# An earlier start for the tokens, a warm-up and split key folds in an attention and mixture-of-experts kernel

## Chip, cores and metric

One core of one Trainium2 chip. Times are device microseconds of one execution; lower is better. TensorE is called PE, VectorE DVE, ScalarE ACT, GpSimd POOL; SP is the engine that only issues transfers.

## What is computed

A transformer block on 2048 tokens of width 512, all in float32:

```python
h  = x + LinearAttention(layernorm(x)) @ wo
h2 = h + MoE(layernorm(h))            # top-1 of 8 experts, width 1792, silu
# attention, for each of 32 heads of width 16:
phi(q) = concat(softmax(q @ w_phi), softmax(-(q @ w_phi)))   # the same for k
o = phi_q @ (phi_k^T V) / (phi_q @ sum(phi_k))
# MoE: out = sum_e gate_e * silu(x @ w1[e]) @ w2[e] for the one expert with the largest logit;
# the softmax over that single logit is 1
```

## The kernel before

Tokens come in 16 tiles of 128. Each float32 product is made of three matmuls in a faster format: every operand is split into a high part (`hi_of`, a rounding copy on ACT, L69) and a low part (`lo_of`, a subtraction on DVE, L72), and `mm3` (L75 to L77) adds hi·hi, hi·lo and lo·hi. A split is therefore one ACT and one DVE instruction, and PE waits for both.

**Stage 1, weights.** `w_phi` is folded into the query and key weights: `fold` (L300) makes, for each of four row blocks `dt`, four full float32 matmuls into one PSUM bank `pf` (in the trace each is two records) and then splits that bank into `wkhi` and `wklo` (or `wqhi`, `wqlo`). Value weights (`split_w` into `wvhi`, `wvlo`) and output weights (`wohi`, `wolo`) are only split, with the gate's columns beside them. Raw weights are loaded in two halves each (`load_w`, L297) on SP's queue, in this order: w_phi, key weights, first tokens, gate, value weights, second tokens, query weights, output weights, transposed output weights.

**Stage 2, tokens.** For tile `c`: `s_ln` loads it (`load_x`, L216) and normalises it (DVE statistics L220 and L221, POOL for the reciprocal root, ACT for `xn`, L230); `s_tr` transposes it on PE (L235, into `pt`) and splits it (`xh`, `xl`); `s_k`, `s_v` and `s_q` project it; `feat1` and `feat2` make the two softmaxes (DVE, ACT, and on POOL the product `ph`, L352); `s_kv` accumulates phi_k^T V, `s_qt` transposes the query features into `phT` (L375 and L376). The last two tiles' query features are finished in the next stage.

**Stage 3, attention output and routing**, a loop over `c` (L562) in which each step works on four tiles at different depths: `s_num` (pn, L265), `s_ot` (pto), `s_wo` (po), routing ranks, and from `c` = 12 on the splits of the first expert's weights. `fq` of tiles 14 and 15 is made at `c` = 2 and 3, and their `s_qt` runs at `c` = 3 and 4.

**Stage 4, experts**: units of 128 tokens, each with its expert's weights loaded, split and multiplied.

The order on each engine is set by a scheduler that takes the written program and moves independent instructions; `tc.issue_after(ins)` keeps instructions of the same engine behind `ins` in that order, and makes no wait between engines. Pools hand out buffers in turn: `ps` has four PSUM banks for `bank(...)` tiles, `psw` one double bank for `pv` and `po`.

Of the kernel before, what the change touches and what calls it, by code (L numbers as in the profile page):

```python
# [9 lines left out]
F32 = mybir.dt.float32  # L10
# [4 lines left out]
AF = mybir.ActivationFunctionType  # L15
# [6 lines left out]
P = 128  # L22
# [19 lines left out]
def kernel(  # L42
# [22 lines left out]
    def mid(ap, n):  # L65
        return ap.unsqueeze(1).to_broadcast([ap.shape[0], n] + list(ap.shape[1:]))

    def hi_of(dst, src):
        A.activation(dst, src, AF.Copy)  # L69

    def lo_of(dst, src, hi):
        V.tensor_tensor(dst, src, hi.bitcast(F32), op=OP.subtract)  # L72

    def mm3(ps, ahi, alo, bhi, blo, first, last):
        T.matmul(ps, ahi, bhi, start=first, stop=False)  # L75
# [45 lines left out]
    def bank(name):  # L121
        return ps.tile([P, 512], F32, name=name, tag="b")
# [65 lines left out]
    with ExitStack() as actx:  # L188
# [22 lines left out]
        def row(name, bufs, tag):  # L211
            return work.tile([P, D], F32, name=name, tag=tag, bufs=bufs)

        def load_x(c):
            st[c]["xt"] = row("xt", 3, "xt")
            nc.sync.dma_start(st[c]["xt"], x[c * P:(c + 1) * P, :])  # L216

        def ln_rstd(src, mv, rstd):
            bs = work.tile([P, 6], F32, name="bs")
# [9 lines left out]
            G.tensor_scalar(nb, mean, rstd, -1.0, op0=OP.mult, op1=OP.mult)  # L229
            A.activation(dst, src, AF.Identity, bias=nb, scale=rstd)  # L230

        def transpose4(src, name):
            pt = bank(name)
            for k in range(KD):
                T.transpose(pt[:, k * P:(k + 1) * P], src[:, k * P:(k + 1) * P], ident)  # L235
            return pt.rearrange("p (k t) -> p k t", k=KD)
# [42 lines left out]
        if True:  # L279
# [15 lines left out]
            def load_w(i, src):  # L295
                for j in range(2):
                    nc.sync.dma_start(stage[i][j], src[j * 256:(j + 1) * 256].rearrange("(t p) d -> p t d", p=P))  # L297
                return stage[i]

            def fold(w_raw, whi, wlo):  # L300
                for dt in range(KD):
                    pf = bank("pf")
                    for t in range(4):
                        T.matmul(pf[:, t * P:(t + 1) * P], w_raw[t // 2][:, t % 2, dt * P:(dt + 1) * P],
                                 wphi_s[:, t, :], start=True, stop=True)
                    hi_of(whi[:, dt, :], pf)
                    lo_of(wlo[:, dt, :], pf, whi[:, dt, :])

            def split_w(w_raw, gate, whi, wlo):
                for t in range(KD):  # L310
# [7 lines left out]
                    lo_of(wlo[:, :, i, v], gate[:, :, i, :], whi[:, :, i, v])  # L318

            def s_ln(c):  # L320
                load_x(c)
                xt = st[c]["xt"]
                mv = work.tile([P, 2], F32, name="mv", bufs=4)
                rstd = work.tile([P, 1], F32, name="rstd", bufs=4)
                std = work.tile([P, 1], F32, name="std", bufs=4)
                ve = ln_rstd(xt, mv, rstd)
                G.tensor_tensor(std, ve, rstd, op=OP.mult)
                st[c]["std"], st[c]["mv"] = std, mv
                st[c]["xn"] = row("xn", 3, "xn")
                normalise(st[c]["xn"], xt, mv[:, 0:1], rstd)  # L330

            def s_tr(c):
                st[c]["x"] = split_t(transpose4(st[c]["xn"], "pt"))
# [22 lines left out]

            def s_v(c):
                p = proj2(st[c]["x"], wvhi, wvlo, "pv")
                A.activation(v17[c % 3].rearrange("p (i h) f -> p i h f", i=2)[:, :, :, 0:DH],
                             p[:, :, 0:D // 2].rearrange("p i (h f) -> p i h f", f=DH), AF.Copy)  # L360
                A.activation(xwg[:, c], p[:, :, D // 2:HC], AF.Copy, scale=st[c]["std"])

# [7 lines left out]
            def s_qt(c):  # L370
                ph = st[c]["fq"]
                for i in range(2):
                    pt = bank("ptq")
                    for g in range(4):
                        T.transpose(pt[:, g * P:(g + 1) * P], ph[:, (4 * i + g) * P:(4 * i + g + 1) * P], ident)  # L375
                    A.activation(phT[c][:, 4 * i:4 * i + 4, :], pt.rearrange("p (g t) -> p g t", g=4), AF.Copy)  # L376

            nc.sync.dma_start(wphi_s, wphi.rearrange("t p f -> p t f"))
            wk_raw = load_w(0, wqkT[D:2 * D])
            s_ln(0)  # L380
            nc.sync.dma_start(wgs, wg.rearrange("(t p) e -> p t e", p=P))
            wv_raw = load_w(1, wv)
            s_ln(1)
            wq_raw = load_w(2, wqkT[0:D])
            wo_raw = load_w(3, wo)
            for i in range(3):
                V.memset(v17[i][:, :, DH:DH + 1], 1.0)
            fold(wk_raw, wkhi, wklo)
            woT_raw = load_w(0, woT)
            s_tr(0)  # L390
            split_w(wv_raw, wgs.rearrange("p t (i e) -> p t i e", i=2), wvhi, wvlo)
            pc = bank("pcs")
            for k in range(KD):
                T.matmul(pc[:, 0:E], onesf, wgs[:, k, :], start=(k == 0), stop=(k == KD - 1))
            wgc = wp.tile([P, KD, E], F32, name="wgc")
            csg = wp.tile([P, E], F32, name="csg")
            V.tensor_scalar(csg, pc[:, 0:E], 1.0 / D, None, op0=OP.mult)
            V.tensor_tensor(wgc, wgs, mid(csg, KD), op=OP.subtract)

            def s_k(c):  # L400
                return proj(st[c]["x"], wkhi, wklo, "pk")
# [4 lines left out]
            for c in range(NT - 1):  # L406
                pk = s_k(c)
                if c:
                    st[c - 1]["fq"] = feat2(st[c - 1]["tq"])
                tk = feat1(pk)  # L410
                s_v(c)
                if c == 0:
                    fold(wq_raw, wqhi, wqlo)
                if c == 3:
                    pg = bank("pog")
                    for dt in range(KD):
                        for t in range(4):
                            T.matmul(pg[:, dt * E:(dt + 1) * E], woT_raw[t // 2][:, t % 2, dt * P:(dt + 1) * P],
                                     wgc[:, t, :], start=(t == 0), stop=(t == 3))
                    split_w(wo_raw, pg[:, 0:KD * E].rearrange("p (t i e) -> p t i e", t=KD, i=2), wohi, wolo)  # L420
                if c + 2 < NT:
                    s_ln(c + 2)
                s_tr(c + 1)
                if c == NT - 2:
                    st[c]["fk"] = feat2(tk)
                    tk = feat1(s_k(NT - 1))
                    s_v(NT - 1)
                    s_kv(c - 1)
                    s_qt(c - 1)
                    st[NT - 1]["fk"] = feat2(tk)  # L430
                    pq = [proj(st[i]["x"], wqhi, wqlo, "pq") for i in (NT - 2, NT - 1)]
                else:
                    pq = proj(st[c]["x"], wqhi, wqlo, "pq")
                    st[c]["fk"] = feat2(tk)
                    st[c]["tq"] = feat1(pq)
                    if c:
                        s_kv(c - 1)
                        s_qt(c - 1)
# [123 lines left out]
        for c in range(NT + 8):  # L562
            if c > 1:
                at(s_num, c)
                at(s_ot, c - 1)
            if c in (2, 3):
                st[NT - 4 + c]["fq"] = feat2(st[NT - 4 + c]["tq"])
            if c in (3, 4):
                s_qt(NT - 5 + c)
            if c == 5:  # L570
                c1.close()
                mw = ctx.enter_context(tc.tile_pool(name="mw", bufs=1, reuse_waits="tile"))
                raw.extend(mw.tile([P, CW], F32, name=f"raw{i}") for i in range(4))
            at(s_wo, c - 2)
            b, j = divmod(c - 3, NB)
            if j == NB - 1:
                at(s_inv, b - 1, NT // NB)
                if b == NT // NB // 2:
                    s_first()
                at(s_top, b, NT // NB)  # L580
                if b == NT // NB // 2 - 1:
                    s_star()
                    late[0].close()
                    mwb = ctx.enter_context(tc.tile_pool(name="mwb", bufs=1, reuse_waits="tile"))
                    first_expert(mwb)
# [273 lines left out]
```

## Time and profile before

| | us |
|---|---|
| median of three runs (lowest to highest) | 724.08 (721.95 to 724.55) |
| the profiled execution, its own time | 722.81 |
| its span, first to last instruction | 721.0 |
| PE busy in the span | 697.6 |
| DVE busy | 450.6 |
| ACT busy | 324.2 |
| POOL busy | 171.7 |

The profile is one execution. Busy time of an engine is the time in which at least one of its instructions ran; idle time is put down to what ended it. A matmul's record is longer than the step to the next one, since matmuls overlap; the step between starts is its price in a stream. The clock column is the share of PE's full clock that was granted; before the first recorded change of the clock it shows 1.00.

### The profile page before, as it was taken

How to read it: one execution, taken by the hardware profiler on the slowest of the kernel's cores; microseconds unless marked ns; L12 is line 12 of the kernel's file. 1: busy time of each engine (PE TensorE's matmuls, PEld its weight loads, DVE VectorE, ACT ScalarE, POOL GpSimd, SP SyncE). 2: the span in 40 equal slices, each digit the busy share in tenths (PEclk: the TensorE clock that was granted, in tenths of full speed). 3: DMA queues.
4: the chain of work that ended last, by engine and by line, in shares of the span. 5: the costliest groups of instructions: out<-in, count | busy, mean ns of one | idle time of the engine just before them, and what ended most of it. 6: DMA issues, size and time to landing. Idle time of an engine off the chain costs nothing. (4 is left out here: it accounts for less than half of the span.)

```text
span 721.0 us, 12308 instructions
## 1 busy us (share of the span) xinstructions
PE 697.6 (97%) x4130; PEld 606.6 (84%) x4130; DVE 450.6 (63%) x886; ACT 324.2 (45%) x522; POOL 171.7 (24%) x271
## 2 busy tenths in 40 slices
PE   5999999999999999879999999999999999999996
PEld 5889998989999999758888888888888888888885
DVE  3987888777785679784422999972284563922211
ACT  3544444443324347442112888861284553822211
POOL 2255535433315435531110011111011111011110
PEclk9999999999999999999999999999999999999999
DMA  8210101000002249318400799981065481001000
GB/s 310 85 30 31 45 15 30 15 30 1 1 2 74 74 141 398 136 44 310 174 31 7 278 362 396 359 349 36 15 239 218 145 320 32 1 29 31 30 31 5
DMA packets 21910, 87.59 MB, mean 121 GB/s; under 512 B 3071, under 2 KB 3583, under 8 KB 14657
## 3 DMA queue, kind: packets, MB, share of 16 engines
q1 hardware_dynamic: 18624, 76.86, 29.1%
q0 software_dynamic: 3200, 9.75, 4.0%
q8 instruction: 34, 0.56, 0.3%
q14 instruction: 52, 0.42, 0.2%
HBM read 78.18 MB, written 9.21 MB: 121 GB/s over the span
## 5 line engine op out<-in xcount | busy, mean ns | idle before, releaser
L72 DVE TENSOR_TENSOR wlo<-raw,whi 128x1024 fp32r<-128x1024 f32 (+1 forms) x120 | 135.9, 1151 | 15.8 <-ACT whi L69 8.1
L69 ACT ACTIVATE whi<-raw 128x1024 fp32r<-128x1024 f32 (+1 forms) x120 | 118.1, 1001 | 60.4 <-PE mh L77 43.6
L75 PE MATMUL mh<-whi,xhi 128*128 128x512 f32 (+1 forms) x304 | 114.6, 377 | 0.2 <-ACT xhi L69 0.2
L76 PE MATMUL mh<-wlo,xhi 128*128 128x512 f32 (+1 forms) x304 | 111.2, 366 | 0.0
L77 PE MATMUL mh<-whi,xlo 128*128 128x512 f32 (+1 forms) x304 | 111.2, 366 | 0.0
L76 PE MATMUL my<-wlo,hThi 128*128 128x512 f32 x266 | 104.9, 394 | 3.5 <-DVE wlo L72 3.3
L75 PE MATMUL my<-whi,hThi 128*128 128x512 f32 x266 | 107.7, 405 | 0.2 <-ACT hThi L69 0.2
L77 PE MATMUL my<-whi,hTlo 128*128 128x512 f32 x266 | 104.7, 394 | 0.3 <-DVE hTlo L72 0.3
L803 POOL DMA_INDIRECT out_dram<-yo,sidx x19 | 21.5, 1131 | 347.9 <-DVEq L640 198.9
L72 DVE TENSOR_TENSOR hTlo<-mtr,hThi 128x512 fp32r<-128x512 f32 x76 | 47.0, 621 | 88.7 <-ACTq L640 54.9
L163 ACT ACTIVATE hs<-mh 128x512 f32<-128x512 f32 x76 | 41.0, 540 | 132.4 <-PE mh L77 132.4
L352 POOL TENSOR_TENSOR ph<-t,sm 128x1024 f32<-128x1024 f32 x32 | 62.1, 1941 | 79.4 <-DVE sm L350 39.4
L77 PEld LDWEIGHTS mh<-whi,xlo 128*128 128x128 f32 x304 | 57.0, 188 | 10.3
L75 PEld LDWEIGHTS mh<-whi,xhi 128*128 128x128 f32 x304 | 57.1, 188 | 9.9 <-ACT xhi L69 0.5
L76 PEld LDWEIGHTS mh<-wlo,xhi 128*128 128x128 f32 x304 | 57.2, 188 | 9.3
L76 PEld LDWEIGHTS my<-wlo,hThi 128*128 128x128 f32 x266 | 50.3, 189 | 14.4 <-DVE wlo L72 4.1
L802 DVE SCALAR_TENSOR_TENSOR yo<-my,xg 128x512 f32<-128x512 f32 x19 | 14.2, 748 | 75.2 <-PE my L77 75.2
L77 PEld LDWEIGHTS my<-whi,hTlo 128*128 128x128 f32 x266 | 50.2, 189 | 11.1 <-DVE hTlo L72 0.5
L75 PEld LDWEIGHTS my<-whi,hThi 128*128 128x128 f32 x266 | 50.3, 189 | 9.9 <-ACT hThi L69 0.5
L69 ACT ACTIVATE hThi<-mtr 128x512 fp32r<-128x512 f32 x76 | 41.1, 542 | 11.7 <-PE mtr L732 11.6
L349 DVE TENSOR_REDUCE sm<-t 128x64 f32<-128x1024 f32 x32 | 38.8, 1214 | 10.3 <-ACT t L344 10.3
L344 ACT ACTIVATE t<-t 128x1024 f32<-128x1024 f32 x32 | 33.9, 1060 | 21.3 <-DVE t L343 17.3
(209 smaller groups left out, 1382.1 us busy)
## 6 DMA issues: line engine op xcount, KB each, us to landing
raw<-in_w_dram SPq DMA_DIRECT2D x56, 1024.0 KB, 5.3
xt<-in_x_dram SPq DMA_DIRECT2D x32, 256.0 KB, 2.8
hbuf<-hb SPq DMA_DIRECT2D x8, 516.0 KB, 3.2
phT<-in_wqkT_dram SPq DMA_DIRECT2D x4, 512.0 KB, 6.9
phT<-in_wv_dram SPq DMA_DIRECT2D x2, 512.0 KB
phT<-in_wo_dram SPq DMA_DIRECT2D x2, 512.0 KB, 8.4
phT<-in_woT_dram SPq DMA_DIRECT2D x2, 512.0 KB, 6.9
xg<-hbuf,gidx POOLq DMA_INDIRECT x21, 3.8
```

Source lines behind the costliest of these rows:

```text
L69: A.activation(dst, src, AF.Copy)
L72: V.tensor_tensor(dst, src, hi.bitcast(F32), op=OP.subtract)
L75: T.matmul(ps, ahi, bhi, start=first, stop=False)
L76: T.matmul(ps, ahi, blo, start=False, stop=False)
L77: T.matmul(ps, alo, bhi, start=False, stop=last)
L163: A.activation(hs[c % 2][:, 0:fw], p[:, 0:fw], AF.Silu)
L344: A.activation(t, t, AF.Exp)
L349: V.tensor_reduce(sm, t, AX.X, OP.add)
L352: G.tensor_tensor(ph.rearrange("p (a f) -> p a f", f=DH), t, bc(sm, DH), op=OP.mult)
L802: V.scalar_tensor_tensor(y, py, g[:, D + 2:D + 3], g[:, 0:D], op0=OP.mult, op1=OP.add)
L803: G.indirect_dma_start(out=out, out_offset=bass.IndirectOffsetOnAxis(ap=sidx[:, u:u + 1], axis=0), in_=y, in_offset=None, bounds_check=S - ...
```

## The change

1. The first two token tiles are loaded on ACT's queue, ahead of everything else; SP's queue begins with w_phi and the key weights.
2. PE runs 28 transposes of the identity matrix into an unused bank (`warm`).
3. The key weights are folded in two halves, one for each half of the load: all four `dt` for the first half, then the transposes and split of the first token tile (in the `psw` bank), then all four `dt` for the second half with the splits.
4. The value splits, the second tile's normalisation and what belongs to the gate are kept behind the last key split on ACT and on DVE. Their loads are on SP and are not held.
5. The output weights' splits are kept behind the copy of the third tile's `v` on ACT.
6. `s_qt` of tiles 14 and 15 runs at `c` = 4 and 5.

```diff
-        def load_x(c):
+        def load_x(c, queue=nc.sync):
             st[c]["xt"] = row("xt", 3, "xt")
-            nc.sync.dma_start(st[c]["xt"], x[c * P:(c + 1) * P, :])
+            queue.dma_start(st[c]["xt"], x[c * P:(c + 1) * P, :])
...
+            def fold_half(w_raw, pf, dt, i):
+                for t in (2 * i, 2 * i + 1):
+                    T.matmul(pf[:, t * P:(t + 1) * P], w_raw[i][:, t % 2, dt * P:(dt + 1) * P],
+                             wphi_s[:, t, :], start=True, stop=True)
+
+            def fold_split(pf, dt, whi, wlo):
+                return hi_of(whi[:, dt, :], pf), lo_of(wlo[:, dt, :], pf, whi[:, dt, :])
...
             def s_ln(c):
-                load_x(c)
+                if c > 1:
+                    load_x(c)
...
+            load_x(0, nc.scalar)
+            load_x(1, nc.scalar)
+            s_ln(0)
             nc.sync.dma_start(wphi_s, wphi.rearrange("t p f -> p t f"))
             wk_raw = load_w(0, wqkT[D:2 * D])
-            s_ln(0)
-            nc.sync.dma_start(wgs, wg.rearrange("(t p) e -> p t e", p=P))
-            wv_raw = load_w(1, wv)
-            s_ln(1)
-            wq_raw = load_w(2, wqkT[0:D])
-            wo_raw = load_w(3, wo)
+            warm = bank("warm")
+            for i in range(28):
+                T.transpose(warm[:, i % 4 * P:(i % 4 + 1) * P], ident, ident)
...
-            fold(wk_raw, wkhi, wklo)
-            woT_raw = load_w(0, woT)
-            s_tr(0)
-            split_w(wv_raw, wgs.rearrange("p t (i e) -> p t i e", i=2), wvhi, wvlo)
...
+            pf = [bank("pf") for _ in range(KD)]
+            for dt in range(KD):
+                fold_half(wk_raw, pf[dt], dt, 0)
+            st[0]["x"] = split_t(transpose4(st[0]["xn"], "pt", psw.tile([P, 2, 512], F32, name="pt0", tag="w")[:, 0, :]))
+            for dt in range(KD):
+                fold_half(wk_raw, pf[dt], dt, 1)
+                hi, lo = fold_split(pf[dt], dt, wkhi, wklo)
+            with tc.issue_after(hi.ins), tc.issue_after(lo.ins):
+                nc.sync.dma_start(wgs, wg.rearrange("(t p) e -> p t e", p=P))
+                wv_raw = load_w(1, wv)
+                split_w(wv_raw, wgs.rearrange("p t (i e) -> p t i e", i=2), wvhi, wvlo)
+                s_ln(1)
+                wq_raw = load_w(2, wqkT[0:D])
+                wo_raw = load_w(3, wo)
+                woT_raw = load_w(0, woT)
...
-                    split_w(wo_raw, pg[:, 0:KD * E].rearrange("p (t i e) -> p t i e", t=KD, i=2), wohi, wolo)
+                    with tc.issue_after(st[2]["v"].ins):
+                        split_w(wo_raw, pg[:, 0:KD * E].rearrange("p (t i e) -> p t i e", t=KD, i=2), wohi, wolo)
...
-            if c in (3, 4):
-                s_qt(NT - 5 + c)
+            if c in (4, 5):
+                s_qt(NT - 6 + c)
```

More of the change, by code (lines that the diff above doesn't have):

```diff
@@ L68, in hi_of @@
     def hi_of(dst, src):
-        A.activation(dst, src, AF.Copy)
+        return A.activation(dst, src, AF.Copy)
     def lo_of(dst, src, hi):
-        V.tensor_tensor(dst, src, hi.bitcast(F32), op=OP.subtract)
+        return V.tensor_tensor(dst, src, hi.bitcast(F32), op=OP.subtract)
     def mm3(ps, ahi, alo, bhi, blo, first, last):
@@ L230, in normalise, with transpose4 @@
             A.activation(dst, src, AF.Identity, bias=nb, scale=rstd)
-        def transpose4(src, name):
-            pt = bank(name)
+        def transpose4(src, name, pt=None):
+            pt = bank(name) if pt is None else pt
             for k in range(KD):
@@ L302, in fold @@
                     pf = bank("pf")
[L303 to L307, printed above, removed]
+                    fold_half(w_raw, pf, dt, 0)
+                    fold_half(w_raw, pf, dt, 1)
+                    fold_split(pf, dt, whi, wlo)
             def split_w(w_raw, gate, whi, wlo):
@@ L358, in s_v @@
                 p = proj2(st[c]["x"], wvhi, wvlo, "pv")
-                A.activation(v17[c % 3].rearrange("p (i h) f -> p i h f", i=2)[:, :, :, 0:DH],
+                st[c]["v"] = A.activation(v17[c % 3].rearrange("p (i h) f -> p i h f", i=2)[:, :, :, 0:DH],
                              p[:, :, 0:D // 2].rearrange("p i (h f) -> p i h f", f=DH), AF.Copy)
@@ L385 @@
-            wo_raw = load_w(3, wo)
+            warm = bank("warm")
+            for i in range(28):
+                T.transpose(warm[:, i % 4 * P:(i % 4 + 1) * P], ident, ident)
             for i in range(3):
                 V.memset(v17[i][:, :, DH:DH + 1], 1.0)
-            fold(wk_raw, wkhi, wklo)
-            woT_raw = load_w(0, woT)
-            s_tr(0)
-            split_w(wv_raw, wgs.rearrange("p t (i e) -> p t i e", i=2), wvhi, wvlo)
-            pc = bank("pcs")
-            for k in range(KD):
-                T.matmul(pc[:, 0:E], onesf, wgs[:, k, :], start=(k == 0), stop=(k == KD - 1))
@@ L395 @@
[L395 to L398, printed above, removed]
+            pf = [bank("pf") for _ in range(KD)]
+            for dt in range(KD):
+                fold_half(wk_raw, pf[dt], dt, 0)
+            st[0]["x"] = split_t(transpose4(st[0]["xn"], "pt", psw.tile([P, 2, 512], F32, name="pt0", tag="w")[:, 0, :]))
@@ new lines @@
+            for dt in range(KD):
[9 more added lines that the diff above has]
+                woT_raw = load_w(0, woT)
+                pc = bank("pcs")
+                for k in range(KD):
+                    T.matmul(pc[:, 0:E], onesf, wgs[:, k, :], start=(k == 0), stop=(k == KD - 1))
+                wgc = wp.tile([P, KD, E], F32, name="wgc")
+                csg = wp.tile([P, E], F32, name="csg")
+                V.tensor_scalar(csg, pc[:, 0:E], 1.0 / D, None, op0=OP.mult)
+                V.tensor_tensor(wgc, wgs, mid(csg, KD), op=OP.subtract)
```

## The prediction

> **What bounds the kernel now.** I read the page first, then the list of what TensorE (PE) waited for, then the start in order of time, then busy time by stretch.
>
> ```profile
> PE 697.6 (97%) x4130; PEld 606.6 (84%) x4130; DVE 450.6 (63%) x886; ACT 324.2 (45%) x522; POOL 171.7 (24%) x271
> ```
>
> ```profile
> PE pf L304 <- DMA phT<-in_wqkT_dram: 6.7, 2, 5.5
> PE my L76 <- DVE wlo L72: 3.3, 1, 3.3
> PE po L75 <- DVE lg L467: 2.6, 2, 2.1
> PE ptq L375 <- POOL hb L461: 1.4, 1, 1.4
> PE pt L235 <- DVE wklo L72: 1.0, 1, 1.0
> ```
>
> PE is the bound: 697.6 of 721.0 us. Its idle time stands in a few places, and the change touches three of them: the first wait for the key weights (6.7 us), the first transpose (1.0) and the late query transpose (1.4). What is gained there reaches the end only if PE is full from there on.
>
> ```profile
> 25.00:27.50 2.50, 2.50 (x18) 2.27 (x18) 2.50 (x5) 2.14 (x4) 0.00 (x0) 1.00 0.00 0
> 27.50:30.00 2.50, 2.30 (x10) 1.54 (x10) 2.50 (x7) 0.00 (x0) 0.97 (x3) 1.00 0.00 0
> 50.00:60.00 10.00, 10.00 (x79) 9.46 (x77) 9.25 (x15) 4.66 (x7) 3.99 (x6) 1.00 0.04 5
> ```
>
> Columns: stretch, its length, busy us (count) of PE, PEld, DVE, ACT, POOL, PE clock, DMA share, GB/s. Up to 30 us VectorE (DVE) is as full as PE, so the start is a race of two engines. Later PE alone is full (50 to 60), though DVE has little to spare. The waits listed for 30 to 200 us are nil, so what the start gains is carried to there one for one.
>
> Now the start itself, in order of time (start, length, engine, line, tiles, count):
>
> ```profile
> 1.27 0.29 POOL masks.py:199 TENSOR_SCALAR_AFFINE_SELECT ident<-ident 128x128 f32<-128x128 f32 x1
> 5.51 2.04 PE L304 MATMUL pf<-wphi_s,phT 128*128 128x128 f32 x8 [5.51 <-DMA phT<-in_wqkT_dram]
> 8.78 4.62 PE L304 MATMUL pf<-wphi_s,phT 128*128 128x128 f32 x24 [1.22 <-DMA phT<-in_wqkT_dram]
> 9.52 0.69 DVE L220 BATCH_NORM_STATS2 bs<-xt 128x6 f32<-128x512 f32 x1 [7.36 <-DMA xt<-in_x_dram]
> 12.29 0.81 ACT L230 ACTIVATE xn<-xt,nbias,rstd 128x512 f32<-128x512 f32 x1 [2.36 <-POOL nbias L229]
> 13.01 2.04 ACT L69 ACTIVATE wkhi<-pf 128x512 fp32r<-128x512 f32 x4
> 14.37 0.66 PE L235 MATMUL pt<-ident,xn 128*128 128x128 f32 x4 [0.97 <-DVE wklo L72]
> 17.28 1.90 DVE L72 TENSOR_TENSOR wvlo<-phT,wvhi 128x512 fp32r<-128x512 f32 x3
> 19.62 0.39 PE L77 MATMUL pk<-wkhi,xl 128*128 128x512 f32 x1
> 22.60 3.29 PE L304 MATMUL pf<-wphi_s,phT 128*128 128x128 f32 x28
> 29.20 0.40 PE L77 MATMUL pq<-wqhi,xl 128*128 128x512 f32 x1
> 29.44 0.39 PE L75 MATMUL pk<-wkhi,xh 128*128 128x512 f32 x1
> 32.24 0.28 PE L75 MATMUL pv<-wvhi,xh 128*128 128x260 f32 x1
> 32.36 0.28 PE L76 MATMUL pv<-wvlo,xh 128*128 128x260 f32 x1
> ```
>
> Three things are seen. The key weights land in halves, at 5.5 and 8.8 us, and the first tokens at 9.5, behind them. The fold (L304; each matmul of the program is two records) costs 2.04/8 = 0.25 us a record at first, 0.19 in the second burst, and 3.29/28 = 0.12 later: the early records run on about half the clock, though the clock column (1.00) doesn't show it before 12 us. And tokens and key weights come ready together only at 13 to 14 us. A split, projection and fold step starts every 0.51 us on ACT (2.04/4), 0.60 on DVE (1.90 for three), 0.24 on PE for 512 columns (29.20 to 29.44) and 0.12 for 260 (32.24 to 32.36).
>
> **The change, part by part.** *Tokens on ScalarE's queue.* ACT has nothing to do there; the table load behind the two issues is hidden under the 2.8 us between the landing and xn (9.52 to 12.29). By when do the loads land?
>
> ```profile
> 2.50:5.00 2.50, 0.00 (x0) 0.00 (x0) 0.00 (x0) 0.00 (x0) 0.00 (x0) 1.00 0.94 324
> 5.00:7.50 2.50, 1.99 (x8) 1.78 (x8) 0.00 (x0) 0.00 (x0) 0.00 (x0) 1.00 0.93 273
> 7.50:10.00 2.50, 1.28 (x6) 1.22 (x6) 0.48 (x1) 0.21 (x1) 0.00 (x0) 1.00 1.02 357
> ```
>
> DMA moves some 300 GB/s from 2.5 us on. If the first tokens (0.26 MB) share it with the equal wphi load, both are in by 2.5 + 0.52 MB/324 GB/s = 4.1; I take 4.5, and xn 3.6 later (9.52 to 13.10), at 8.1. The two token tiles ahead of the key weights cost these nothing at best and 0.52 MB/300 = 1.7 us at worst: halves at 5.5 to 7.2 and 8.8 to 10.5; I take 6.5 and 9.4.
>
> *Warm-up: 28 transposes,* from ident (1.6) on. Their price at half clock:
>
> ```profile
> 292.20:295.60 3.40, 3.40 (x18) 3.40 (x18) 1.79 (x7) 0.81 (x2) 1.94 (x5) 0.50 0.83 246
> 295.13 0.85 PE L147 MATMUL mtr<-ident,xn 128*128 128x128 f32 x4
> 295.81 0.60 PE L235 MATMUL pto<-ident,o 128*128 128x128 f32 x4
> ```
>
> 0.85/4 = 0.21 each at half clock, 0.60/4 = 0.15 at full. So 28 x 0.21 = 5.9 us, ending at 7.6 (5.9 at the fast price, 8.8 at the fold's 0.25). PE was idle until 5.5, so 1.1 us at most of it lies past the landing I take for the first half, and is paid for by faster records behind it if they raise the clock. In the before trace the clock rose at about 12.3, after 3.5 us of unbroken matmuls from 8.78.
>
> *Fold in halves, with the token transpose between.* First half: 16 records x 0.12 from 7.6, to 9.5; at half clock it would be 16 x 0.21 = 3.4. The transpose, queued on PE ahead of the second half, has xn since 8.1: 9.5 to 10.0. Second half, landed at 9.4: 10.0 to 11.9 (before: 13.4). ACT then does xh (10.2 to 10.7) and four wkhi (to 12.8); DVE does xl (to 11.4) and four wklo of 0.60 (to 13.8). What is queued behind: the value splits, now strictly after the key splits on both engines: wvhi on ACT to 14.9 and its gates to 15.2, wvlo and gates on DVE to 16.4.
>
> *PE behind that.* The order of the built program has the 12 key matmuls first, at the pace of wklo (0.60 a group of three against 0.71 on PE), about 11.9 to 14.7; before they ended at 19.9. Then one value matmul, which needs ACT's gates (15.2), ten fold records of the query weights (1.2; their load has no landing row: 3.95 MB are ahead of its end and PE used it at 17 us before, so I take 15.8 and 0.5 us of new wait) to 16.5; 23 value matmuls x 0.12, to 19.3; 22 fold records x 0.12, to 21.9; the next transposes 0.5; 12 query matmuls x 0.24, to 25.2. The same point before is 29.44. DVE must have the last query split ready by 24.5 and the next xl by 25.2: from 10.8 it has some 22 pieces of 0.60, to 24.1, so it keeps up by about 1 us. Gain 4.2; I take off 0.2 for the third and fourth token tiles, which now come up in DVE's order some 4 us earlier: 4.0 (range 2.5 to 5.5).
>
> *Wo splits held back* behind the third tile's v.
>
> ```profile
> L72 DVE TENSOR_TENSOR wolo<-phT,wohi 128x512 fp32r<-128x512 f32 x4 | 2.7, 678 | 0.0
> 20.01 2.18 ACT L69 ACTIVATE wohi<-phT 128x512 fp32r<-128x512 f32 x4
> ```
>
> They are 2.7 us of DVE and 2.2 of ACT; half of the DVE part lay in the crowded start, which the 22 pieces above already leave out. In the new place, near 50 us, DVE is 9.25 of 10 busy; cost 0 to 1.4 if PE is made to wait; I take 0, as PE's own list shows no wait on features there.
>
> *Query tiles 14 and 15 one step later.*
>
> ```profile
> 217.84 1.93 POOL L352 TENSOR_TENSOR ph<-t,sm 128x1024 f32<-128x1024 f32 x1 [15.42 <-DVE den L269]
> 219.83 1.09 PE L375 MATMUL ptq<-ident,ph 128*128 128x128 f32 x8 [1.39 <-POOL hb L461]
> ```
>
> PE waited 1.39 for GpSimd's ph (the memset named came right after it). In the new order four pn and the 24 po matmuls (2.9 us) stand ahead of these transposes; they wait for nothing new, so 1.4 goes (0 to 1.5). All else on PE stands in the same order.
>
> **Sum.** 4.0 + 1.4 = 5.4 us off the span: 715.6, and off the profiled execution's own 722.81: 717.4. The median of the three runs (724.08) is 1.3 above that execution, which would give 718.7. I forecast 718.0, between them.
>
> One thing moves with the shift:
>
> ```profile
> 288.80:292.20 3.40, 1.34 (x12) 1.37 (x12) 3.40 (x8) 0.73 (x2) 2.99 (x7) 1.00 0.04 14
> 319.50:322.90 3.40, 1.28 (x6) 1.05 (x6) 3.37 (x12) 0.00 (x0) 2.19 (x2) 1.00 0.00 0
> 322.90:326.30 3.40, 3.40 (x10) 2.41 (x9) 2.38 (x7) 0.00 (x0) 1.08 (x1) 0.51 0.57 155
> ```
>
> Twice a 3.4 us stretch in which PE was under 40% busy is followed by one at half clock, about 1.7 us lost each time. Where such stretches begin after the shift I can't tell: up to 1.7 either way.
>
> **Rivals.** *Transposes don't raise the clock.* Then the first half of the fold runs at 0.21, to 11.0, the transposes to 11.9, and the clock rises, as before, 3.5 us or more into unbroken matmuls, about 12 to 14. Second half to about 14.4, wklo 2.5 to 3 us later, PE's 25.2 becomes 28.0: gain 1.4 + 1.4 = 2.8, 720.0. For it: no stretch of this trace holds more than eight transposes in a row, so none shows them waking the clock. Against it: 295.13 and 295.81 show them following the clock as matmuls do. The Trainium skill ("TensorE: Matmul & The Clock Gate", Part 4: PE-mode transpose) speaks for this rival: it says the full clock doesn't engage for transposes, which don't count as busy in the same way; the trace neither shows nor refutes that. Chance 0.16.
>
> *The loads share, and the shared ones come late.* Key halves at 7.2 and 10.5, query weights and the third and fourth tokens late too: the fold's end moves 0.6, DVE stalls another 1 to 1.5: gain 2 + 1.4 = 3.4, 719.4. Chance 0.12. The Trainium skill ("DMA: Bandwidth & Descriptors", Issuing engines are not separate DMA queues) has it that loads issued by several engines run on the same 16 DMA engines and interleave; by it the worse landings above hold, not the better.
>
> *Slower: the tokens land late and block PE.* The transpose stands on PE ahead of the second half of the fold. Before, token loads took this long:
>
> ```profile
> DMA to landing us min/median/max: 8.0/8.3/8.7
> ```
>
> Issued at 0.9 they would land at 9.5 at that latency: xn at 13.1, PE idle from 9.5 to 13.1 with the second half behind it, half clock again as after 288.8: second half 13.6 to 16.9, PE's 25.2 becomes about 30.9, a loss of 1.5 that the late tiles' 1.4 just cancels. That landing, 9.5, is the point from which it decides; each us later costs one, and at 12 it gives +2.6: 725.4. For it: that latency row. Against it: before, the tokens stood behind 1.3 MB on one queue, and here they stand first on another. Chance 0.07.
>
> **How the numbers follow.** The forecast case has 0.65. Its own range is 714.2 (gain 5.5 + 1.4 and a half-clock stretch of 1.7 gone, from 722.8) to 720.5. The range that holds 8 in 10 must take in most of the first two rivals, with the median's 1.3 above the profiled execution: 714.2 to 721.6. About 0.5% (3.6 us) is what a measurement of this kernel can tell from no change. Faster by more: 0.65 x 0.85 and a third of the two middle rivals, 0.64. Within: 0.28. Slower: the last rival and its like, 0.08.
>
> **What would show it.** In the changed kernel's trace: 28 transposes from about 1.7 to 7.6 or earlier; the fold's first half at 0.12 a record right behind them; the first token statistics on DVE near 4.5; the last key matmul near 14.5; the second tile's key matmuls starting near 25, not 29.4; no wait of ptq on POOL near 215. I am wrong on the start if fold records stay at 0.21 to 0.25 until 12 us, if PE waits for xn with the transpose at its head, or if DVE's query splits make PE wait past 25; and wrong on the carrying if new waits stand between 30 and 200 us.

## The result and the profile after

| | before | after |
|---|---|---|
| median, us (lowest to highest) of four runs each | 723.32 (721.95 to 724.55) | 717.61 (716.77 to 718.33) |
| ratio of the times, with its 95% interval | | 0.9924 (0.9908 to 0.994) |
| the profiled execution, its own time and span, us | 722.81, 721.0 | 716.77, 715.1 |

The change gains 5.7 us. The forecast was 718.0, a gain of 5.4 on the sum.

The page's busy line, and then rows of PE's list of waits (total, times, longest), both after:

```profile
PE 698.8 (98%) x4158; PEld 609.3 (85%) x4158; DVE 452.4 (63%) x886; ACT 324.4 (45%) x522; POOL 167.5 (23%) x271
```

```profile
PE my L76 <- DVE wlo L72: 3.3, 1, 3.3
PE po L75 <- DVE lg L486: 3.0, 2, 2.1
PE warm L392 <- POOL ident masks.py:199: 1.6, 1, 1.6
PE pcs L412 <- DVE wklo L72: 0.2, 1, 0.2
PE pf L302 <- DMA phT<-in_wqkT_dram: 0.2, 1, 0.2
```

The wait for the key weights went from 6.7 us to 0.2; the 1.0 at the first transpose and the 1.4 of `ptq` are not in the list. PE's busy time rose by 1.2 us: 5.6 us of warm-up, against 2.7 us less for the key folds (6.66 to 3.97) and some less elsewhere. The start of the changed kernel, in order of time (start, length, engine, line, tiles, count, idle time before):

```profile
1.61 5.63 PE L392 MATMUL warm<-ident 128*128 128x128 f32 x28 [1.61 <-POOL ident masks.py:199]
4.56 0.69 DVE L220 BATCH_NORM_STATS2 bs<-xt 128x6 f32<-128x512 f32 x1 [2.41 <-DMA xt<-in_x_dram]
7.33 0.81 ACT L230 ACTIVATE xn<-xt,nbias,rstd 128x512 f32<-128x512 f32 x1 [1.44 <-POOL nbias L229]
7.42 2.02 PE L302 MATMUL pf<-wphi_s,phT 128*128 128x128 f32 x16 [0.18 <-DMA phT<-in_wqkT_dram]
9.28 0.60 PE L235 MATMUL pt<-ident,xn 128*128 128x128 f32 x4
9.72 1.95 PE L302 MATMUL pf<-wphi_s,phT 128*128 128x128 f32 x16
11.16 2.48 DVE L72 TENSOR_TENSOR wklo<-pf,wkhi 128x512 fp32r<-128x512 f32 x4
11.89 1.06 PE L412 MATMUL pcs<-wgs,onesf 128*128 128x8 f32 x8 [0.22 <-DVE wklo L72]
12.81 0.48 PE L75 MATMUL pk<-wkhi,xh 128*128 128x512 f32 x1
15.46 0.39 PE L77 MATMUL pk<-wkhi,xl 128*128 128x512 f32 x1
25.37 0.39 PE L75 MATMUL pk<-wkhi,xh 128*128 128x512 f32 x1
```

Warm-up, first half, transposes, second half and key matmuls stand one behind the other with 0.4 us of waiting in all. The second tile's key matmuls begin at 25.37, not 29.44.

How far the same instruction stands from its place before, along the span (start times in the two traces, us):

| | before | after | offset |
|---|---|---|---|
| first key matmul of the second tile | 29.44 | 25.37 | −4.07 |
| a `kvps` matmul of the fourth tile | 50.73 | 46.66 | −4.07 |
| first `pn` of the attention output | 206.83 | 204.37 | −2.46 |
| 121st `po` record, behind the late query tiles | 242.19 | 238.10 | −4.09 |
| first matmul of the experts (`mh`) | 296.66 | 291.06 | −5.60 |
| end of the span | 721.01 | 715.07 | −5.94 |

The gain of the start was cut by 1.6 us between 50 and 207 us and the late tiles gave 1.6. The changed kernel's busy time by stretch shows the cut (columns as in the prediction: busy us and count of PE, PEld, DVE, ACT, POOL, then the clock):

```profile
30.00:50.00 20.00, 20.00 (x134) 18.09 (x133) 18.32 (x31) 12.03 (x20) 8.69 (x12) 1.00 0.11 27
54.26:57.68 3.42, 3.42 (x34) 3.42 (x33) 2.49 (x4) 0.75 (x2) 1.30 (x1) 1.00 0.00 0
57.70:61.10 3.40, 3.40 (x12) 2.81 (x12) 1.61 (x5) 1.80 (x4) 1.75 (x5) 0.50 0.00 0
```

And the row of the same stretch in order of time:

```profile
54.11 3.63 PE L436 MATMUL pog<-wgc,phT 128*128 128x8 f32 x32
```

PE is busy all the time, yet from 57.7 on it runs 3.4 us at half clock. Right ahead of that stand the 32 `pog` records (the gate's columns of the output weights), which stream only 8 columns each. Before, the same burst stood at 58.18 and no such stretch followed.

### The profile page after: what moved, and what is told of

Read it like the earlier page. It is cut to its first block, busy times and chain, and to the rows that moved or that the text cites. A ratio compares the mean times of both kernels' runs of the same rounds, so it can differ in the third digit from the quotient of the medians.

```text
span 715.1 us, 12363 instructions
## 1 busy us (share of the span) xinstructions
PE 698.8 (98%) x4158; PEld 609.3 (85%) x4158; DVE 452.4 (63%) x886; ACT 324.4 (45%) x522; POOL 167.5 (23%) x271
## 5 line engine op out<-in xcount | busy, mean ns | idle before, releaser
L356 DVE TENSOR_REDUCE sm<-t 128x64 f32<-128x1024 f32 x32 | 38.8, 1215 | 10.4 <-ACT t L351 10.2
```

The lines of the kernel that those rows point to most:

```text
L356: V.tensor_reduce(sm, t, AX.X, OP.add)
```

## The experiments

The theory: each of the six parts works as the prediction's sum has it, and the clock is raised by columns streamed through PE. The rivals differ by part and stand in each expectation. Diffs are against the changed kernel, where not said otherwise. Where one time is given it is one execution; the kernels before that ran beside them had medians of 722.64 us (e1 to e4) and 722.43 us (e9 to e11), and one run of 724.15 us (e5 to e8).

**e1: only the late query tiles move**, against the kernel before.

```diff
-            if c in (3, 4):
-                s_qt(NT - 5 + c)
+            if c in (4, 5):
+                s_qt(NT - 6 + c)
```

> The kernel before with the move of the two late query tiles alone. My theory: PE's wait of ptq on POOL (1.4 us) goes and nothing takes its place, so from 225 us on PE stands 1.4 to 1.6 us earlier than before and the start is as before (second tile's key matmuls at 29.4). Time 1.5 us under before, unless a half-clock stretch moves, which is worth 1.7 either way. Rival: the wait only hid another one (the next po or pn waits instead) and PE is at the same place at 225 us.

Median 721.28 us of ten runs, 1.36 under before, ratio 0.9981 (0.9962 to 0.9999). PE's list has no `ptq` row any more. From the first `pn` to the 121st `po` record it took 33.76 us (208.24 to 242.00) against 35.36 before: 1.60. The profiled run ended only 0.85 us earlier, since it had a half-clock stretch at 61.66, right behind `pog`, that the profiled run before had not.

**e2: one warm-up transpose instead of 28.**

```diff
-            for i in range(28):
+            for i in range(1):
                 T.transpose(warm[:, i % 4 * P:(i % 4 + 1) * P], ident, ident)
```

> The changed kernel with 1 warm-up transpose in place of 28; every engine's order is otherwise the same. The first half of the key weights landed at 7.3 us in the changed kernel, so PE begins the fold at 7.3 in both. My theory: without the 28 the fold's records cost 0.21 until the clock rises after 10.7 us or later, the transposes and the second half come 1.6 to 2.5 us later, and the second tile's key matmuls start at 27 to 28 instead of 25.4; time 1.5 to 2.5 us over the changed kernel. Rival (DVE's chain sets the start, not PE's clock): they start at 25.4 to 26 all the same.

Its start in order of time:

```profile
7.42 3.38 PE L302 MATMUL pf<-wphi_s,phT 128*128 128x128 f32 x16 [5.34 <-DMA phT<-in_wqkT_dram]
10.64 0.60 PE L235 MATMUL pt<-ident,xn 128*128 128x128 f32 x4
26.73 0.40 PE L75 MATMUL pk<-wkhi,xh 128*128 128x512 f32 x1
```

The first half starts at the same 7.42 and takes 3.38 us, not 2.02: 0.21 a record, the half-clock price. So it was the transposes that woke the clock. The loss at the second tile is only 1.36 us, less than expected (26.73 against 27 to 28), since the clock rises at 10.27 already. Median 720.45 (ten runs), ratio 0.9962 (0.9947 to 0.9976) against 0.9924 with the warm-up: 2.8 us over the changed kernel's 717.61 (2.4 over its 718.06 in e11), where 1.5 to 2.5 were expected. That is more than the 1.36; in this profile the half-clock stretch behind `pog` also lasts 6.8 us instead of 3.4.

**e3: a warm-up of the same length with 8 columns instead of 128.**

```diff
-            for i in range(28):
-                T.transpose(warm[:, i % 4 * P:(i % 4 + 1) * P], ident, ident)
+            for i in range(14):
+                T.matmul(warm[:, 0:8], ident, ident[:, 0:8], start=True, stop=True)
```

> The changed kernel with 14 matmuls of 8 columns (28 records) in place of the 28 transposes. Theory A (what wakes the clock is columns streamed, not records): the clock does not rise before some full-width work has run, the fold's records cost 0.21, and the second tile's key matmuls start at 27 to 28 as with one transpose. Rival B (any stream of records counts as busy): the clock rises at 5 to 8.5 us and they start at 25.4.

Its start:

```profile
1.61 6.14 PE L392 MATMUL warm<-ident 128*128 128x8 f32 x28 [1.61 <-POOL ident masks.py:199]
7.61 3.76 PE L302 MATMUL pf<-wphi_s,phT 128*128 128x128 f32 x16
11.16 1.06 PE L235 MATMUL pt<-ident,xn 128*128 128x128 f32 x4
27.98 0.39 PE L75 MATMUL pk<-wkhi,xh 128*128 128x512 f32 x1
```

6 us of unbroken PE records did not raise the clock: the fold behind them runs at half clock, the clock rises at 13.04, and the start loses 2.6 us. That this is more than with a single transpose is the place of the clock's windows (last section): the window in which the fold began ended at 9.63 here, with 2.0 us of fold in it, and in e2 at 10.27, with 2.85. One execution: 720.95.

**e4: `pog` twice over**, 64 records instead of 32.

```diff
-                    for dt in range(KD):
+                    for dt in [i % KD for i in range(2 * KD)]:
```

> The changed kernel with the 16 pog matmuls (8 columns each, 32 records, 3.6 us) done twice, 7.2 us in a row. The changed kernel's trace has a half-clock stretch of 3.4 us right behind them, which before had not. Theory A (8-column matmuls count as idle, and the stretch comes when they fill one 3.4 us window): at least one whole window is now filled, so a half-clock stretch must follow, or already begin among them; PE loses 3.6 for the extra work. Rival B (the stretch had another cause): with the work shifted there is no half-clock row between 50 and 70 us, and only 3.6 us are added.

The burst in order of time, then the stretches from there on:

```profile
54.10 11.08 PE L436 MATMUL pog<-wgc,phT 128*128 128x8 f32 x64
```

```profile
57.50:61.00 3.50, 3.50 (x18) 3.50 (x18) 0.00 (x0) 0.00 (x0) 0.80 (x1) 0.50 0.00 0
61.00:64.50 3.50, 3.50 (x18) 3.50 (x18) 0.00 (x0) 0.00 (x0) 0.00 (x0) 0.50 0.00 0
64.50:68.00 3.50, 3.50 (x13) 3.07 (x13) 1.91 (x6) 1.80 (x4) 0.70 (x2) 0.50 0.00 0
```

32 more records, which took 3.6 us before, make the burst 7.5 us longer: the clock stays at half for 13.7 us (56.93 on), though PE has a record running at every moment. Narrow matmuls hold the clock down. One execution: 726.05.

**e5: tokens first, but on SP's queue.**

```diff
-            load_x(0, nc.scalar)
-            load_x(1, nc.scalar)
+            load_x(0)
+            load_x(1)
```

> The changed kernel with the two token loads first on SP's queue in place of ACT's; the order of every engine's work is otherwise the same. Theory A (the second queue saves only issue time on SP, and the bytes are the same): w_phi and the key weights are issued 0.9 us later, their first half lands at 7.3 to 8.2, and the second tile's key matmuls start at 25.4 to 26.3. Rival B (the second queue also moves the bytes in parallel): the tokens land first and the key weights clearly later, over 1.5 us, and they start at 27 or later.

Its start:

```profile
8.64 2.02 PE L302 MATMUL pf<-wphi_s,phT 128*128 128x128 f32 x16 [2.18 <-DMA phT<-in_wqkT_dram]
22.92 0.69 DVE L220 BATCH_NORM_STATS2 bs<-xt 128x6 f32<-128x512 f32 x1 [2.20 <-DMA xt<-in_x_dram]
24.35 0.63 PE L235 MATMUL pt<-ident,xn 128*128 128x128 f32 x4 [0.83 <-DVE t L350]
27.76 0.39 PE L75 MATMUL pk<-wkhi,xh 128*128 128x512 f32 x1
```

The fold begins 1.22 us later, at 8.64; the second tile's key matmuls 2.4 us later, because the third token tile is late too (DVE waits 2.20 us for it, PE 0.83 for what DVE then has to do first). That lies between the two theories. The second part is not shown to be the queue's: the order of SP's loads also came out differently. The third tile's load is issued at 13.34, behind both loads of the transposed output weights; in the changed kernel it is issued at 8.86, ahead of them. What the queue itself is worth is the 1.22 us, near the 0.87 us that SP needs here to issue the two token loads. The Trainium skill ("DMA: Bandwidth & Descriptors", Issuing engines are not separate DMA queues) has it that loads of several engines share the same DMA engines, and that a second issuing engine saves only the time to issue them. The trace agrees, with 1.22 against 0.87 us. One execution: 721.84.

**e6: tokens on SP behind the key weights**, where they stood before, with the rest of the change kept.

```diff
-            load_x(0, nc.scalar)
-            load_x(1, nc.scalar)
-            s_ln(0)
             nc.sync.dma_start(wphi_s, wphi.rearrange("t p f -> p t f"))
             wk_raw = load_w(0, wqkT[D:2 * D])
+            load_x(0)
+            load_x(1)
+            s_ln(0)
```

> The changed kernel with the two token loads on SP's queue behind the key weights, so that the tokens land late as in the kernel before. Theory A (the transpose stands on PE ahead of the second half, as the prediction's slower rival has it): the tokens land at 8 to 9, xn 3.6 later, PE waits for it, and the second tile's key matmuls start 2 to 4 us later than 25.4, at 27.5 to 29.5. Rival B (the key weights, landing earlier without the tokens ahead, set the start): they start within 1 us of 25.4.

Its start, then the same time by stretch:

```profile
8.83 0.69 DVE L220 BATCH_NORM_STATS2 bs<-xt 128x6 f32<-128x512 f32 x1 [6.68 <-DMA xt<-in_x_dram]
12.46 0.66 PE L235 MATMUL pt<-ident,xn 128*128 128x128 f32 x4 [3.23 <-ACT xn L230]
12.96 2.91 PE L302 MATMUL pf<-wphi_s,phT 128*128 128x128 f32 x16
31.30 0.39 PE L75 MATMUL pk<-wkhi,xh 128*128 128x512 f32 x1
```

```profile
10.30:13.70 3.40, 1.24 (x11) 1.24 (x12) 0.00 (x0) 1.35 (x3) 1.10 (x4) 1.00 1.05 402
13.73:17.10 3.37, 3.37 (x19) 3.37 (x17) 3.14 (x5) 2.86 (x7) 0.00 (x0) 0.50 1.06 387
17.10:20.50 3.40, 3.40 (x10) 2.73 (x10) 3.40 (x10) 1.69 (x5) 0.00 (x0) 0.50 1.00 361
```

This is the prediction's slower rival made on purpose: the transpose stands at PE's head and waits 3.23 us for `xn`, the clock falls for 6.8 us, and the second tile comes at 31.30, which is 1.9 us later than before and 5.9 later than with tokens first. I had expected 2 to 4. One execution: 720.70, still under before, by the late tiles (1.6) and the half-clock stretch of before at 292 (1.9), which this run did not have.

**e7: whole fold ahead of the transposes.**

```diff
             for dt in range(KD):
                 fold_half(wk_raw, pf[dt], dt, 0)
+                fold_half(wk_raw, pf[dt], dt, 1)
...
             for dt in range(KD):
-                fold_half(wk_raw, pf[dt], dt, 1)
                 hi, lo = fold_split(pf[dt], dt, wkhi, wklo)
```

> The changed kernel with the key weights folded whole (both halves of each row block together, the token transpose behind all of it). Theory A (the halves are worth little now that the tokens are early, since PE and DVE only swap xl and wklo): PE waits about 0.9 us for the second half among the fold, the key matmuls start 0.5 to 1 us later than 12.8, and the second tile's at 25.4 to 26.2. Rival B (folding in halves carries the gain): the second tile's start at 27 or later.

The first key matmul stands at 13.28, 0.5 later, as theory A has it; the second tile's at 27.36, 2.0 later, theory B's number. The order on PE changed as well: records of the query fold stand among the key matmuls, and the query matmuls wait 0.42 and 0.20 for `wqlo`. So the 2.0 cannot be put down to the halves alone. One execution: 719.26.

**e8: the output weights' splits not held.**

```diff
-                    with tc.issue_after(st[2]["v"].ins):
+                    if True:
                         split_w(wo_raw, pg[:, 0:KD * E].rearrange("p (t i e) -> p t i e", t=KD, i=2), wohi, wolo)
```

> The changed kernel without holding the output weights' splits back. In the order that comes out, two of them stand on ACT and DVE ahead of the first token tile's split, though their load lands only at about 15.7 us in the changed kernel. Theory A (these engines take their work strictly in order): ACT and DVE stop there until about 16 us, xh and all behind it come 6 us later, and the second tile's key matmuls start at 30 to 33. Rival B (the hold only moves DVE work of 1.2 us out of the crowded start): 25.4 to 26.8.

The list of ACT's waits, and one stretch:

```profile
ACT wohi L69 <- DMA phT<-in_wo_dram: 7.6, 1, 7.6
```

```profile
13.40:20.00 6.60, 1.52 (x8) 1.52 (x8) 4.06 (x7) 4.72 (x10) 0.00 (x0) 0.50 1.01 373
```

Two of these splits moved ahead of the first token split on ACT and waited 7.6 us there for a load that stands near the end of SP's queue. Everything behind them waited, PE ran dry, and the clock was at half from 13.39 for 10.2 us. The second tile's key matmuls came at 34.33, 9.0 us late, against 30 to 33 expected. One execution: 723.72.

**e9: `pog` in four portions**, one row block per step, each with its own two small splits.

```diff
-                    for dt in range(KD):
-                        for t in range(4):
-                            T.matmul(pg[:, dt * E:(dt + 1) * E], woT_raw[t // 2][:, t % 2, dt * P:(dt + 1) * P],
-                                     wgc[:, t, :], start=(t == 0), stop=(t == 3))
...
+                if 3 <= c < 3 + KD:
+                    dt, v = c - 3, slice(D // 2, HC)
+                    pg = bank("pog")
+                    for t in range(4):
+                        T.matmul(pg[:, 0:E], woT_raw[t // 2][:, t % 2, dt * P:(dt + 1) * P],
+                                 wgc[:, t, :], start=(t == 0), stop=(t == 3))
```

> The changed kernel, but the gate columns of the output weights (pog, 32 records of 8 columns in a row at 54 us) are made in four portions of 8 records, one each at c = 3 to 6. Theory A (a run of 8-column matmuls that fills one of the clock's windows halves the clock for the next 3.4 us, which cost 1.6 us at 57.7): no row at clock 0.50 between 50 and 70 us; the offset against the kernel before stays at -4.0 to 200 us; time 716.0, 1.6 under the changed kernel. Theory B (the clock falls there because of something else, or falls elsewhere instead, since windows move against the program): a row at 0.50 remains between 50 and 75 us, or a new one stands elsewhere; time 717.0 to 718.0. The six added small splits are 6 x 0.2 us of ACT and DVE beside a full PE: at most 0.5 us.

The first portion in order of time, and the stretch where the clock had been at half:

```profile
54.12 0.95 PE L443 MATMUL pog<-wgc,phT 128*128 128x8 f32 x8
```

```profile
57.40:60.80 3.40, 3.40 (x30) 3.23 (x28) 3.15 (x7) 1.92 (x3) 2.18 (x5) 1.00 0.01 2
```

No half-clock stretch between 50 and 70 us; the first `pn` starts at 202.59, 4.24 under before, so the start's gain now arrives whole. Median 715.65 of six runs, 2.4 under e11, ratio to before 0.9911 (0.9877 to 0.9946). 1.8 us of the 2.4 stand at the first `pn`.

**e10: e9, and three small things at the start.** The second tile's load on SP behind the key weights, 24 transposes, the gate's column sums (`pcs`) later.

```diff
-            load_x(1, nc.scalar)
...
             wk_raw = load_w(0, wqkT[D:2 * D])
+            load_x(1)
             warm = bank("warm")
-            for i in range(28):
+            for i in range(24):
...
+                if c == 1:
+                    pc = bank("pcs")
+                    for k in range(KD):
+                        T.matmul(pc[:, 0:E], onesf, wgs[:, k, :], start=(k == 0), stop=(k == KD - 1))
```

> The changed kernel with pog in four portions, the second token tile's load on SP behind the key weights, 24 warm-up transposes for 28, and the column sums of the gate (pcs, 8 records that end 0.9 us after the first wklo) moved to c = 1. Theory A (three small prices add): the first key half lands near 6.6 instead of 7.3, the first key matmul stands at 11.3 to 11.9 instead of 12.8, the second tile's key matmuls at 24.0 to 24.8 instead of 25.4, and with no half-clock stretch near 58 the time is 714.5 to 716. Theory B (as where the tokens were on SP: a token tile that comes later on SP makes DVE and PE wait in the crowded start): first key matmul earlier, second tile's at 25.4 or later, with PE waiting for xn or t before it; time 716 to 718.5.

Its start:

```profile
6.79 2.17 PE L302 MATMUL pf<-wphi_s,phT 128*128 128x128 f32 x16
11.40 0.50 PE L75 MATMUL pk<-wkhi,xh 128*128 128x512 f32 x1 [0.23 <-DVE wklo L72]
23.54 0.39 PE L75 MATMUL pk<-wkhi,xh 128*128 128x512 f32 x1
```

Median 714.48 of six runs (713.92 to 715.48), ratio 0.9888 (0.9854 to 0.9921): the lowest median of all, and its runs don't overlap with those of the changed kernel beside it (e11). The first key matmul is 1.4 us earlier, as expected, and the second tile's 1.8, more than expected. But much of this is only order: the `kvps` matmul of the fourth tile stands at 46.12, 0.54 earlier. PE is full from there on, so the 0.9 us of `pcs` that were moved out of the start were paid behind it. Theory A had the time right (714.48, at the edge of 714.5 to 716) and the reason half wrong; the three things were not taken apart, and e9's runs reach down to 714.30, so what they add to e9 is not settled.

**e11: the changed kernel again.**

> The changed kernel once more, for the comparison with the two others of this call. Both theories: 717.6 (716.8 to 718.5), 0.992 of the kernel before; half-clock stretches near 57 and 317 us if the clock's windows stand as before against the program, others if they run free.

Median 718.06 of eleven runs (717.08 to 719.45), ratio 0.9937 (0.9916 to 0.9958). Against the sixteen runs of the kernel before beside it (722.43) that is a gain of 4.4 us, less than the 5.7 of the four runs in the result; the two intervals overlap. One stretch of its profile:

```profile
286.14:289.55 3.41, 3.40 (x16) 3.41 (x17) 2.96 (x8) 1.36 (x4) 2.56 (x6) 0.50 0.41 143
```

Its half-clock stretches stand at 57.45, 286.14 and 316.86; the changed kernel's first profile had those at 57.68 and 317.09 and none at 286. The granted clock, as a mean over the run, was 0.991 or 0.989 in all eleven runs. In the result's four it was 0.994 in the profiled one and 0.991 to 0.992 in the others. A stretch of 3.41 us at half clock lowers this mean by 0.0024 (1.7 of 716 us); two of them and the fall at the very end of the run (3.1 us at most in these profiles) leave 0.993. So the usual run of the changed kernel has a stretch more than its first profile.

## Why the prediction was right

- **Where the gain is.** As forecast: 4.07 us of the start against 4.0, and 1.63 of the late tiles against 1.4 (a little over its range, 0 to 1.5). The gain of the start stood unchanged at 50 us, and with `pog` spread it reached 207 us: nothing new waits there.
- **The number was helped by luck.** 4.07 + 1.63 is 5.7, and so is the gain of the medians, though on the way the clock took 1.6 us back. The eleven runs of e11 put the gain at 4.4: with the parts right, the end can lie this far off.
- **The start, step by step.** Most steps came within 0.3 us: token statistics 4.56 (4.5), `xn` done 8.14 (8.1), first half of the fold 7.42 to 9.44 (7.6 to 9.5), transposes 9.28 (9.5), second half to 11.67 (11.9), key splits on DVE to 13.64 (13.8), second tile 25.37 (25.2).
- **Errors of the sum cancelled.** The eight `pcs` records between the first key split and the first key matmul were left out of the sum: the key matmuls began at 12.81, not 11.9, and what follows them at 15.69, not 14.7. On the other side the wait of 0.5 us for the gate's split didn't come up, and the query folds and the transposes took 0.4 to 0.5 less than priced. From 1.0 us behind at the end of the key matmuls the start was 0.17 behind at the second tile. The sum also has a slip: its 0.5 us of new wait for the query weights is named but not added (15.2, one value matmul and ten records make 16.5 without it; with it the start's gain would have been 3.5). The wait didn't come up: these weights landed at 14.38, not 15.8.
- **Landings.** The key halves were put at 6.5 and 9.4, and by the landing times of the trace they came at 7.29 and 8.84. The first was 0.8 later than taken and just outside its range (5.5 to 7.2). PE waited 0.18 us for it, since the warm-up ran until 7.24. The second was 0.6 earlier, at the good end of its range.
- **Rival: transposes don't raise the clock.** Fell. With them the fold runs at 0.12 a record from 7.42 on, without them at 0.21. The Trainium skill ("TensorE: Matmul & The Clock Gate", Part 4: PE-mode transpose) says that transposes don't count; here the measurement decides against it.
- **Rival: shared loads come late.** Only its first landing came true (7.29 against its 7.2). The second key half and the query weights came earlier than taken, and the third token tile landed at 17.76, before at 21.80. e5 shows what late loads cost: 2.4 us.
- **Rival: tokens late.** Not here (4.56), and its place and mechanism were shown by e6. Its price was a little low: with e6's landing, 8.8, the prediction's steps give 30.2 for the second tile, and 31.30 was measured; the half clock went on through the key matmuls, to 20.5, which the prediction had only for the second half of the fold.
- **Half-clock stretches, ±1.7.** Three things moved by this much: one stretch came at 57.7 (a loss of 1.6), the one of before at 292.2 was missing in the profiled run after (a gain of about 1.5), and the third stayed. That they nearly cancelled was chance: e11, the same kernel, has a stretch at 286 (the last section says why the first profile had none). The ±1.7 was the right size, but I looked for the cause in idle PE alone and did not see that a burst of narrow matmuls does the same.
- **Holding the output splits, cost 0.** The offset still stood at −4.07 where `pog` begins (58.18 before, 54.11 after), behind the four large splits, and at −4.24 at 202 us in e9: nothing measurable. What it prevents was large (e8), which the prediction didn't price.

Taken out one at a time, the parts cost 1.4 (warm-up), 2.4 (queue, with the changed order of SP's loads), 5.9 (tokens first), 2.0 (halves) and 9.0 us (hold) at the second tile, in a start that gained 4.1 in all. They are not shares of the gain: each part needs the others.

What stays open: how much of e7's loss is due to the order that came with it, how much of e5's to the order of SP's loads, and the 0.6 us by which e9 gains more than the stretch. The granted clocks (0.992 to 0.996 in e9's runs, 0.989 or 0.991 in e11's) suggest that in some of e9's runs a further stretch fell away; one run of each was profiled, so this is not shown.

## What to carry to other kernels

Price a start as a chain of who comes last on each engine, and ask of every part that is moved earlier what it needs and what it leaves standing at the head of a queue: a step that waits in front (e6, e8) costs its wait and then the fallen clock. Where PE has nothing to do before its first weights, real-width transposes of a constant pay for themselves; narrow ones don't. Where a burst of narrow matmuls stands in a full stream, scatter it, and where PE is full, don't count work as gained that was only moved.

## What the runs showed of the hardware

**The clock counts columns, not records.** 28 transposes of 128 columns raised it; in the changed kernel this happened while they ran. The busy time of the warm-up's records alone, by stretch (PE, PEld, then the clock):

```profile
2.00:4.20 2.20, 2.20 (x12) 2.20 (x11) 1.00 0.83 253
4.20:6.40 2.20, 2.20 (x13) 2.20 (x12) 1.00 1.06 378
6.40:7.30 0.90, 0.84 (x7) 0.60 (x5) 1.00 1.06 379
```

12 or 13 records in 2.2 us, then 7 in 0.9, so the pace goes up near 6.4; the trace's clock record has the rise at 6.48 (the column shows 1.00 until the first change). 28 records of 8 columns raised nothing (e3), and 64 of them kept the clock down (e4). These are full float32 matmuls like the records of the fold, which raised the clock in e2, so it is the width that differs and not the kind.

**The clock is set at the ends of fixed windows of 3.41 us, which stand differently in each execution.** In the first profile after, the rise at 6.48, the fall at 57.68 and the fall at 317.09 stand on one raster: the falls come 15 and 91 times 3.413 us after the rise. In e11 the rise at 6.25 and the falls at 57.45, 286.14 and 316.86 (15, 82 and 91 times 3.413 later) stand on one too, 0.23 us earlier against the program.

**A window need be neither full nor empty.** With the windows of each trace placed by its first rise, the `pog` burst filled three quarters or more of the window ahead of a fall: all of it after (54.27 to 57.68) and in e1, 2.58 of 3.41 us in e2, and shares between these in e3, e4, e5, e7 and e11. In the kernel before, in e6 and in e8 it was split between two windows and filled at most 63% of one (2.15 us in e6); no stretch followed. In the profile before, for instance, a window ended at 60.10, in the middle of the burst (58.18 to 61.81). A rise is alike: PE busy for 2.85 of the 3.41 us up to 10.27 raised the clock in e2, 2.31 of the 3.41 up to 3.92 did not in e9.

**What decided about the stretch at 286.** The same kernel in both, the window that ended last ahead of it:

```profile
282.96:286.37 3.41, 1.77 (x18) 1.51 (x16) 3.41 (x12) 0.81 (x2) 3.08 (x6) 1.00 0.65 265
```

```profile
282.73:286.14 3.41, 1.26 (x12) 0.94 (x11) 3.41 (x14) 0.99 (x3) 3.00 (x7) 1.00 0.71 291
```

Above, in the first profile, PE was busy for 52% of the window and the clock held; below, in e11, for 37%, and it fell. The shift of the raster by 0.23 us is too small for this: on the other's raster the two would have been busy for 2.00 us (first profile) and 1.24 us (e11). What differs is where the work stood. The first of 24 `po` matmuls, in the first profile and then in e11, and the DVE row behind the wait:

```profile
281.38 0.36 PE L75 MATMUL po<-wohi,xh 128*128 128x260 f32 x1 [0.98 <-DVE lg L486]
280.48 0.36 PE L75 MATMUL po<-wohi,xh 128*128 128x260 f32 x1
```

```profile
280.47 0.69 DVE L483 TENSOR_TENSOR hb<-po,xt 128x512 f32<-128x512 f32 x1 [0.88 <-DMA xt<-in_x_dram]
```

In the first profile a token tile came late, DVE waited 0.88 us for it and PE 0.98 for DVE; this moved more of the `po` block into the window and so spared that run the half clock. Of the thirteen profiles this is the only one with that wait. PE was ahead again at the first matmul of the experts, 291.06 against 291.92 in e11.

So one execution can differ from the next by 1.6 us (behind `pog`, after) to 1.9 us (at 292, e6 against before) for each such place without any difference in the work; a difference of that size between two single profiles says nothing until the half-clock stretches of both have been laid side by side.
